# The filter stage of a Hyena and MoE kernel: a turned input, matrix B in an idle half, float32 row tiles, and an earlier first layer

## The chip, the cores and the metric

The kernel runs on one core of one Trainium2 chip. The metric is device time in microseconds (us) of one launch; the kernel before takes 2395.51 us, the median of 3 runs (2389.8 to 2403.55). Engines are named as in the profile: PE is TensorE (its weight loads, PEld, are shown apart), DVE VectorE, ACT ScalarE, POOL GpSimd, and SP the queue that issues most DMAs.

## The reference

Two layers follow each other, and both are computed in float32:

```python
h_mlp = np.maximum(pos_emb @ w1, 0.0) @ w2            # the filter: (S,64) @ (64,64), relu, @ (64,128)
h_filt = h_mlp * np.exp(-0.01 * pos)[:, None]
u = x * v                                             # (4, 11456, 128)
y = irfft(rfft(u, n=2*S) * rfft(h_filt, n=2*S)[None])[:, :S]
out1 = x * y                                          # 45824 tokens of 128
...
e_idx = argmax(out1 @ w_gate + modality_bias[modality_id])
out[token] = gate_w * (relu(out1 @ w1[e_idx]) @ w2[e_idx])      # 8 experts, 128 -> 1024 -> 128
```

The change touches only how the spectrum of `h_filt` is made, and when the first of the four batches of `x` and `v` is read.

## The kernel before, in words

The long convolution is done as a transform in two steps over N1 = 90 and N2 = 64 points. Everything is written as matrix products with constant tables. The program has these stages, in order:

1. **Filter, outer step** (16 steps q, `filter_stages`). A tile of `pos_emb` is loaded (`emb`), turned by four transposes (`pT`, L499) and copied to SBUF by ACT (`pTs`, L501); `hidden` multiplies by `w1` (`m1`, L507), and DVE applies relu and window (`r`, L510); `transform` does the outer transform with the table `whole` (`s`, L520), and ACT copies the result into `A[:, 0]` (L524). The second layer `w2` is not yet applied, since it acts on features and commutes with the transform.
2. **Filter, middle step** (30 groups g of G = 3 frequencies, `filter_middle`). `turn` transposes three slices of `A[:, 0]` (`pa`, L547), ACT copies them (`aT`, L549). `spectrum` multiplies by the table B of the group (`b2`, loaded by SP at L542; result `pz`, L556). Each half of the 128 rows of `pz` holds one of two blocks. ACT rounds both halves (L563) and DVE subtracts (L565), so that `z` holds for each block the rounded part in 64 partitions and the remainder in the other 64. `second` applies `w2` to both blocks with four float32r products (L572, L573) of full height against `ws`, a split of `w2`; ACT and DVE form the three rows of the filter's spectrum `h` (L577, L578, L579), and POOL's queue writes them to `hs` in HBM (L580, 384 KB a group).
3. **Forward step of batch 0** (16 steps q, `forward_stages`): SP loads a tile of `x` and one of `v` (`seq`, L447, 512 KB each); DVE forms `u = x*v` and the sum and difference of its halves (`product`: L452, L455, L456); PE transforms (`s`, L480, here with both blocks in one product of 128 rows); ACT copies into both halves of `A` (L482).
4. The middle step of batch 0 (`middle_stages`, from L615 on), then for each later batch the inverse step of the batch before, routing and the forward step together. From batch 1 on the forward product is done on two halves of 64 rows (L471).
5. The mixture of experts, tile by tile, to the end.

Order of work: PE, ACT, DVE and SP execute in the order in which the program is written. `steps(count, stages)` builds a list of steps from a table such as `"load:0 transform:4 turn:1 hidden:2"`: stage s of item i is written in step i + s, and inside a step in the table's order. `overlapped(first, second, n)` lays the last n steps of one list over the first n of the next. FOUT is the table of stage 1, FMID of stage 2, OUTER of the forward step; F1 = 1 and F2 = 2 are the overlaps between stages 1 and 2, and 2 and 3.

Buffers: `new_a` hands out the next of NA = 11 slots of 4 KB a partition, in turn; who gets a slot waits until its last user is done. Stage 1 takes three slots a step (`emb`, `pTs`, `r`), stage 2 three a group (`b2`, `aT`, `z`), stage 3 two a step (x and v). `ring("h")`, `ring("b")` and `ring("c")` give three places each in the tile `rings`. So `h` of group g waits until the write to `hs` of group g-3 has landed. `bank` gives one of four PSUM banks, `pair` one of two pairs of banks. `A` has two halves; during stages 1 and 2 the kernel before uses only `A[:, 0]`.

## Time and profile before

| what | value |
|---|---|
| median of 3 runs | 2395.51 us (2389.8 to 2403.55) |
| the profiled execution's own time | 2370.12 us |
| its span, first to last instruction | 2367.9 us |
| mean granted TensorE clock | 0.977 |
| PE busy in the span | 95% |
| filter, outer step | 0 to 49.57 us |
| filter, middle step | 49.57 to 120.86 us |
| forward step of batch 0 | 120.86 to 163.74 us |
| the rest | 163.74 to 2367.9 us |

How to read it: the page's shares are of the whole span; the change lies in its first 164 us, which are read with the timeline (instructions in order of time, equal neighbours merged into one row with their count), with the table of windows (busy time of each engine between two times) and with the list of waits. In a timeline row stand the start, the duration of the whole row, engine, line, operation, result<-operands, shape and count, and in brackets how long the engine was idle before and what ended that. A float32 product of PE shows as two records, a float32r product or a transpose as one.

### The profile page before, as it was taken

The page shows a single profiled execution, that of the slowest core. Times are in us where ns is not written, and L with a number is a line of the kernel's source. Part 1 is how long each engine was busy: PE and PEld are TensorE (multiplying, and loading weights), DVE is VectorE, ACT ScalarE, POOL GpSimd, SP SyncE. Part 2 cuts the span into 40 slices and gives each one's busy share as a digit, 9 for nine tenths or more (in the row PEclk, how much of TensorE's full clock was granted, in tenths as well). Part 3 has the DMA queues.
Part 4 walks back from the last instruction along what each step waited for, and adds up shares of the span by engine and source line. Part 5 has one row for each costly group of instructions (what it writes and reads, how often), then busy time and mean ns, then how long its engine had stood idle before and what let it go on. Part 6 is the DMA issues. An engine that isn't in the chain of part 4 may idle for free. (4 is left out here: it accounts for less than half of the span.)

```text
span 2367.9 us, 44124 instructions
## 1 busy us (share of the span) xinstructions
PE 2238.2 (95%) x14826; PEld 1874.1 (79%) x14826; DVE 1839.2 (78%) x3197; ACT 1515.7 (64%) x2969; POOL 994.7 (42%) x987
## 2 busy tenths in 40 slices
PE   8899999899989999899888999999999999999998
PEld 8789966798669966698446777777878888888898
DVE  3789888897788978797566777777777877777797
ACT  5757677577556766576445666666666666666676
POOL 0305400376435755276652554445444333333333
PEclk9999999999899999899998999999999999999999
DMA  3976667677867788575556722112221111111111
GB/s 114 314 298 197 220 223 223 185 226 260 288 209 227 225 285 298 183 222 174 174 163 184 246 68 72 61 62 74 67 62 60 59 46 45 45 46 46 39 41 34
DMA packets 188751, 359.04 MB, mean 152 GB/s; under 512 B 33937, under 2 KB 120285, under 8 KB 188521
## 3 DMA queue, kind: packets, MB, share of 16 engines
q1 hardware_dynamic: 161753, 296.77, 39.5%
q0 software_dynamic: 26608, 59.36, 7.4%
q8 instruction: 120, 1.97, 0.3%
q14 instruction: 110, 0.90, 0.1%
q10 hardware_dynamic: 160, 0.03, 0.0%
HBM read 271.63 MB, written 84.83 MB: 151 GB/s over the span
## 5 line engine op out<-in xcount | busy, mean ns | idle before, releaser
L1072 DVE SCALAR_TENSOR_TENSOR hl<-ph,hh 128x512 fp32r<-128x512 f32 x724 | 499.1, 689 | 249.7 <-ACT hh L1071 147.7
L1071 ACT ACTIVATE hh<-ph 128x512 fp32r<-128x512 f32 x724 | 434.0, 600 | 376.1 <-PE ph L1068 232.1
L1108 POOL DMA_INDIRECT out<-ot,idx x362 | 357.8, 988 | 651.3 <-DVE ot L1105 568.1
L264 POOL DMA_INDIRECT xs<-back,to x360 | 379.6, 1054 | 230.6 <-DVE y L701 81.3
L1066 PE MATMUL ph<-xh,wh 128*128 128x512 f32 (+1 forms) x792 | 304.0, 384 | 2.9 <-ACT wh L1037 2.9
L1089 PE MATMUL po<-hh,wh 128*128 128x512 f32 (+1 forms) x792 | 303.5, 383 | 0.0
L1068 PE MATMUL ph<-xl,wh 128*128 128x512 f32 (+1 forms) x792 | 295.7, 373 | 0.1
L1091 PE MATMUL po<-hl,wh 128*128 128x512 f32 (+1 forms) x792 | 294.9, 372 | 0.0
L1067 PE MATMUL ph<-xh,wl 128*128 128x512 f32 (+1 forms) x792 | 294.5, 372 | 0.0
L1090 PE MATMUL po<-hh,wl 128*128 128x512 f32 (+1 forms) x792 | 293.9, 371 | 0.0
L641 POOL TENSOR_TENSOR more<-more 128x384 f32<-128x384 f32 x112 | 112.4, 1004 | 278.0 <-DVE more L638 233.9
L647 DVE TENSOR_TENSOR part<-pz,rings 128x768 f32<-128x768 f32 x240 | 217.6, 948 | 0.0
L664 PE MATMUL pw<-rings,yT 128*128 128x128 f32 x1440 | 184.4, 279 | 5.4 <-DMA rings<-in_c_bc 5.4
L628 PE MATMUL pz<-rings,aT 128*128 128x128 f32 x1440 | 184.4, 279 | 3.9 <-ACT aT L616 2.3
L664 PEld LDWEIGHTS pw<-rings,yT 128*128 128x128 f32 x1440 | 174.4, 196 | 6.0 <-issue 6.0
L628 PEld LDWEIGHTS pz<-rings,aT 128*128 128x128 f32 x1440 | 174.3, 196 | 5.3 <-ACT aT L616 3.0
L687 PEld LDWEIGHTS wt<-ident,A 128*90 128x90 f32 x1024 | 124.1, 185 | 61.6 <-issue 26.2
L1068 PEld LDWEIGHTS ph<-xl,wh 128*128 128x128 f32 x792 | 149.5, 189 | 27.4 <-DVE xl L1053 0.3
L1091 PEld LDWEIGHTS po<-hl,wh 128*128 128x128 f32 x792 | 149.2, 188 | 27.0
L1066 PEld LDWEIGHTS ph<-xh,wh 128*128 128x128 f32 x792 | 149.7, 189 | 26.3 <-ACT wh L1037 3.3
L1067 PEld LDWEIGHTS ph<-xh,wl 128*128 128x128 f32 x792 | 150.0, 189 | 24.1 <-DVE wl L1038 0.4
L652 POOL TENSOR_TENSOR part<-part,more 128x384 f32<-128x384 f32 x112 | 122.2, 1091 | 110.0 <-DVE part L651 83.1
(186 smaller groups left out, 4426.9 us busy)
## 6 DMA issues: line engine op xcount, KB each, us to landing
seq<-in_x SPq DMA_DIRECT2D x128, 512.0 KB
rings<-in_c_bc SPq DMA_DIRECT2D x240, 192.0 KB
rings<-hs SPq DMA_DIRECT2D x120, 384.0 KB
seq<-in_v SPq DMA_DIRECT2D x64, 512.0 KB
xr<-xo SPq DMA_DIRECT2D x64, 365.6 KB
back<-xr SPq DMA_DIRECT2D x72, 325.0 KB
x<-xs SPq DMA_DIRECT2D x82, 260.0 KB
hs<-rings POOLq DMA_DIRECT2D x30, 384.0 KB
```

Source lines behind the costliest of these rows:

```text
L264: s = pool.indirect_dma_start(out=xs, out_offset=bass.IndirectOffsetOnAxis(ap=ix, axis=0), in_=src, in_offset=None, bounds_check=E * R - 1 ...
L628: pe.matmul(zv[:, blk, :, j], k["aT"][:, blk, D * j:D * j + D], k["b"][:, j, :], start=True, stop=True)
L664: pe.matmul(pw[:, 2 * N2 * j:2 * N2 * (j + 1)], k["yT"][:, blk, D * j:D * j + D], k["c"][:, j, :], start=True, stop=True)
L1066: pe.matmul(p, k[0, "h"][:, f:f + D], k["xh"], start=True, stop=False)
L1067: pe.matmul(p, k[0, "l"][:, f:f + D], k["xh"], start=False, stop=False)
L1068: pe.matmul(p, k[0, "h"][:, f:f + D], k["xl"], start=False, stop=True)
L1071: act.activation(hh, ph, AF.Relu)
L1072: dve.scalar_tensor_tensor(hl, ph, 0.0, hh.bitcast(F32), op0=ALU.max, op1=ALU.subtract)
L1089: pe.matmul(po, k[1, "h"][:, f], hh[:, t], start=g == 0, stop=False)
L1090: pe.matmul(po, k[1, "l"][:, f], hh[:, t], start=False, stop=False)
L1091: pe.matmul(po, k[1, "h"][:, f], hl[:, t], start=False, stop=g == NCH - 1)
L1108: s = pool.indirect_dma_start(out=out, out_offset=bass.IndirectOffsetOnAxis(ap=k["idx"][:, j:j + 1], axis=0), in_=ot[:, j, :], in_offset=N ...
```

## The change

1. `pos_emb` is laid out on the host so that each tile arrives turned. `turn` of stage 1, its four transposes and ACT's copy are gone; `hidden` reads `emb` itself. A step takes two slots instead of three, and the stages move one step closer (FOUT).
2. B of group g is loaded into `A[0:128, 1]`, the half of `A` that is idle in stages 1 and 2, by `load_b(g)`, which is written in step g of the whole program, so it starts with the first step of stage 1. `aT` and `z` live in the rings "b" and "c". Stage 2 takes no slot of `new_a` any more.
3. `second` is two plain float32 products, each with 64 rows: block m uses partitions 64m to 64m+63 of `w2` (it stands in `wf` twice) and of `z`. ACT copies `pz` once over 128 partitions; the split by DVE and the tile `ws` are gone.
4. In FMID the stages of a group stand at steps 0, 1 and 3 instead of 2, 3 and 5 (the load at 1 is gone).
5. The forward step of batch 0 uses the new table FIRST, laid over the last 18 steps of stage 2 (F2 = 18): loads from step 0, `product` 16 and `forward` 17 steps later.

The diff:

```diff
-FOUT = "load:0 transform:4 turn:1 hidden:2"
-FMID = "turn:2 spectrum:3 second:5 load:1"
+FOUT = "load:0 hidden:2 transform:3"
+FMID = "turn:0 spectrum:1 second:3"
+FIRST = "forward:17 load:0 product:16"
...
-F1, F2, F3 = 1, 2, 1
+F1, F2, F3 = 1, 18, 1
...
-        ws = keepp.tile([D, 2, D], F32R, name="ws")
...
-            act.copy(ws[:, 0], wf[:, 0])
-            dve.tensor_sub(ws[:, 1], wf[:, 0], ws[:, 0].bitcast(F32))
...
-            def turn(q):
-                t = kept.pop((q, "emb"))
-                pT = bank("pT")
-                for i in range(4):
-                    pe.transpose(pT[:, D * i:D * i + D], t[:, D * i:D * i + D], ident)
-                pTs = kept[q, 0] = new_a("pTs")[:, 0:512]
-                act.copy(pTs, pT)
-
             def hidden(q):
-                pTs = kept.pop((q, 0))
+                t = kept.pop((q, "emb"))
                 m1 = bank("m1")
                 for i in range(4):
-                    pe.matmul(m1[:, D * i:D * i + D], pTs[:, D * i:D * i + D], wf[:, 1],
+                    pe.matmul(m1[:, D * i:D * i + D], t[:, D * i:D * i + D], wf[:, 1],
                               start=True, stop=True)
...
+        def first_b(g):
+            return A[0:2 * N2, 1].rearrange("p (g j) c n -> p g j (c n)", j=G)[:, g]
+
+        def load_b(g):
+            sp.dma_start(first_b(g),
+                         a["c_bc"][g, :, 0:2 * GK].rearrange("p (j d) -> p j d", j=G))
...
-            def load(g):
-                t = kept[g, "b"] = new_a("b2")[0:2 * N2, 0:2 * GK].rearrange(
-                    "p (j d) -> p j d", j=G)
-                sp.dma_start(t, a["c_bc"][g, :, 0:2 * GK].rearrange("p (j d) -> p j d", j=G))
...
-                aT = kept[g, "aT"] = new_a("aT")[0:2 * N2, 0:G * D]
-                act.copy(aT, pa[0:2 * N2, 0:G * D])
+                aT = kept[g, "aT"] = ring("b")
+                act.copy(aT, pa[:, 0:G * D])
...
-                z = kept[g, "z"] = new_a("z", F32R)[:, 0:4 * GK].rearrange(
-                    "p (b m) -> p b m", b=2)
-                halves = slice(0, 64), slice(64, D)
-                for blk, at in enumerate(halves):
-                    act.copy(z[at, blk], pz[at, 0:2 * GK])
-                for blk, at in enumerate(halves):
-                    dve.tensor_sub(z[halves[1 - blk], blk], pz[at, 0:2 * GK],
-                                   z[at, blk].bitcast(F32))
+                z = kept[g, "z"] = ring("c")
+                act.copy(z, pz[:, 0:2 * GK])
...
                 for m in range(2):
-                    pe.matmul(ph[:, m, 0:2 * GK], ws[:, 0], z[:, m], start=True, stop=False)
-                    pe.matmul(ph[:, m, 0:2 * GK], ws[:, 1], z[:, m], start=False, stop=True)
+                    at = slice(64 * m, 64 * m + 64)
+                    pe.matmul(ph[:, m, 0:2 * GK], wf[at, 0], z[at], start=True, stop=True)
...
-            table = [w.split(":") for w in (LAST if b == nb else OUTER).split()]
+            table = [w.split(":") for w in (LAST if b == nb else OUTER if b else FIRST).split()]
...
         seq = overlapped(steps(NQ, filter_stages()), steps(NG, filter_middle()), F1)
+        for k in range(NG):
+            seq[k] = lambda f=seq[k], k=k: (f(), load_b(k))
...
-        pos.transpose(3, 2, 1, 4, 0, 5).reshape(NQ, D, -1))
+        pos.transpose(3, 0, 5, 4, 2, 1).reshape(NQ, D, -1))
```

How the rows of the engines' orders move, at the three places that matter. First SP, from the program's start: before, 16 loads of `emb` with the constants between, then 30 loads of B, then `seq` (x and v in turn).

```order
L493 DMA emb<-in_pos_emb 128x512 x5
L396 DMA fwd<-in_c_fwd 128x360
L397 DMA inv<-in_c_inv 90x128
L398 DMA small<-in_c_small 128x634
L399 DMA wg<-in_moe_w_gate 128x8
L400 DMA bias<-in_moe_modality_bias 128x16
L493 DMA emb<-in_pos_emb 128x512 x11
L542 DMA b_510<-in_c_bc 128x384
L542 DMA b_518<-in_c_bc 128x384
```

Now the last of `emb`, the end of B and the first of x and v; ahead of these rows `emb` and `A` alternate from the first instruction on.

```order
L490 DMA emb<-in_pos_emb 128x512
L528 DMA A<-in_c_bc 128x384
L490 DMA emb<-in_pos_emb 128x512
L528 DMA A<-in_c_bc 128x384 x15
L444 DMA seq<-in_x 128x1024
L444 DMA seq<-in_v 128x1024
```

B no longer waits behind all of `emb`, and the first x stands right behind the 30th B; it waits for a slot of `new_a`, and 11 such loads find slots that only stage 1 has used.

Second PE, one group in the middle of stage 2, before (`pa` is the turn, `pz` the spectrum, `ph` the second layer):

```order
L547 MATMUL pa<-ident,A 128x128 x3
L556 MATMUL pz<-b_552,aT 128x128 x3
L572 MATMUL ph<-z,ws 128x384
L573 MATMUL ph<-z,ws 128x384
L572 MATMUL ph<-z,ws 128x384
L573 MATMUL ph<-z,ws 128x384
```

and now, with the start of the next group:

```order
L539 MATMUL pa<-ident,A 128x128 x3
L548 MATMUL pz<-A,rings 128x128 x3
L559 MATMUL ph<-rings,wf 128x384 x2
L539 MATMUL pa<-ident,A 128x128 x3
L548 MATMUL pz<-A,rings 128x128 x3
```

Four products of `ph` became two; turn and spectrum stand as they stood.

Third DVE, at the end of stage 2, before (L578 and L579 belong to `second`, L452, L455 and L456 to `product` of the forward step):

```order
L578 TENSOR_TENSOR rings<-ph,rings 128x192
L579 TENSOR_TENSOR rings<-ph,rings 128x192
L452 TENSOR_TENSOR seq<-seq 128x1024
L455 TENSOR_TENSOR seq<-seq 128x512
L456 TENSOR_TENSOR seq<-seq 128x512
```

and now:

```order
L564 TENSOR_TENSOR rings<-ph,rings 128x192
L565 TENSOR_TENSOR rings<-ph,rings 128x192
L449 TENSOR_TENSOR seq<-seq 128x1024
L452 TENSOR_TENSOR seq<-seq 128x512
L453 TENSOR_TENSOR seq<-seq 128x512
L564 TENSOR_TENSOR rings<-ph,rings 128x192
L565 TENSOR_TENSOR rings<-ph,rings 128x192
L449 TENSOR_TENSOR seq<-seq 128x1024
```

The first product stands one group earlier: behind group 28, ahead of group 29, the last.

More of the change, by code (lines that the diff above doesn't have):

```diff
@@ L493, in load, with hidden @@
                 sp.dma_start(t, a["pos_emb"][q])
-            def turn(q):
+            def hidden(q):
                 t = kept.pop((q, "emb"))
-                pT = bank("pT")
-                for i in range(4):
-                    pe.transpose(pT[:, D * i:D * i + D], t[:, D * i:D * i + D], ident)
-                pTs = kept[q, 0] = new_a("pTs")[:, 0:512]
-                act.copy(pTs, pT)
-            def hidden(q):
-                pTs = kept.pop((q, 0))
                 m1 = bank("m1")
                 for i in range(4):
-                    pe.matmul(m1[:, D * i:D * i + D], pTs[:, D * i:D * i + D], wf[:, 1],
+                    pe.matmul(m1[:, D * i:D * i + D], t[:, D * i:D * i + D], wf[:, 1],
                               start=True, stop=True)
@@ L525, in transform @@
                              p[:, h, 0:4 * N1].rearrange("p (n k) -> p k n", n=2))
-            todo = dict(turn=turn, hidden=hidden, transform=transform, load=load)
+            todo = dict(hidden=hidden, transform=transform, load=load)
             return [(int(t), todo[n]) for n, t in (w.split(":") for w in FOUT.split())]
@@ L547, in turn @@
                     pe.transpose(pa[0:2 * N2, D * j:D * j + D], turn_back(g, 0, j), ident)
-                aT = kept[g, "aT"] = new_a("aT")[0:2 * N2, 0:G * D]
-                act.copy(aT, pa[0:2 * N2, 0:G * D])
+                aT = kept[g, "aT"] = ring("b")
+                act.copy(aT, pa[:, 0:G * D])
             def spectrum(g):
-                aT, b2 = kept.pop((g, "aT")), kept.pop((g, "b"))
+                aT, b2 = kept.pop((g, "aT")), first_b(g)
                 pz = bank("pz")
@@ L581, in second @@
                                h[:, :, 1:3].rearrange("p m c k -> p m (c k)"))
-            todo = dict(turn=turn, second=second, spectrum=spectrum, load=load)
+            todo = dict(turn=turn, second=second, spectrum=spectrum)
             return [(int(t), todo[n]) for n, t in (w.split(":") for w in FMID.split())]
@@ L863, in outer_steps @@
                                lambda: (send(NO - 1), places(NO - 1))])
-            table = [w.split(":") for w in (LAST if b == nb else OUTER).split()]
-            return steps(NQ, [(lambda q, t=int(t): min(q + t, NQ + 3) if b < nb else q + t, todo[n])
+            table = [w.split(":") for w in (LAST if b == nb else OUTER if b else FIRST).split()]
+            return steps(NQ, [(lambda q, t=int(t): min(q + t, NQ + 3) if 0 < b < nb else q + t, todo[n])
                               for n, t in table if n in todo])
```

## The prediction

> **What bounds the kernel now.** I read the windows of the first stages, then the timeline of each, then the waits. The table of windows gives, by stage: length, busy time and count for PE, PEld, DVE, ACT, POOL, then granted clock, DMA share and GB/s.
>
> ```profile
> 0.00:49.57 49.57, 43.91 (x320) 43.15 (x321) 11.87 (x21) 23.02 (x51) 3.20 (x11) 1.00 0.40 118
> 49.57:103.48 53.91, 51.04 (x357) 46.77 (x358) 44.12 (x101) 45.24 (x107) 15.54 (x23) 1.00 0.83 260
> 103.48:120.86 17.38, 6.74 (x35) 5.07 (x34) 9.80 (x23) 6.08 (x14) 4.72 (x7) 0.77 1.00 376
> 120.86:163.74 42.88, 42.01 (x256) 41.67 (x256) 36.97 (x46) 25.55 (x32) 0.00 (x0) 0.94 0.92 356
> ```
>
> PE is nearly always busy in the outer step, in most of the middle step and in the forward step. In the third row it is busy for 6.74 of 17.38 us, the DMA engines are full, and the clock falls to 0.77. Here x and v are first read:
>
> ```profile
> 103.34 0.33 SPq L447 DMA_DIRECT2D seq<-in_x  x1
> 115.71 0.33 SPq L447 DMA_DIRECT2D seq<-in_x  x1
> ACT rings L577 <- DMA hs<-rings: 13.3, 12, 2.8
> L580 POOL DMA_DIRECT2D hs<-rings x30: 671/677/688, 57.7 to 119.5; - x30
> 103.48 0.67 POOL L580 DMA_DIRECT2D hs<-rings  x1 [1.14 <-ACT z L563]
> ```
>
> Eleven loads start from 103.34 to 115.71. The 30 writes of h leave between 57.7 and 119.5; the one at 103.48 is the 24th, so 23 intervals before it are 1.99 us each and the 6 after it 2.66 us. ACT's copy for h waits 13.3 us in total for an older write, since h has three places.
>
> From 163.74 us on nothing is changed and what follows starts when the forward step ends; PE is 95% busy over the whole span, so I carry a shift there in full to the end. The profiled execution took 2370.12 us, 25.4 (1.1%) less than the median of the runs, 2395.51. I sum in microseconds against the execution and subtract the same amount from the median.
>
> **Part 1: the outer step loses its turn.**
>
> ```profile
> 6.69 2.04 PE L507 MATMUL m<-wf,pTs 128*128 128x128 f32 x8 [1.10 <-DMA wf<-in_w]
> 10.76 1.39 PE L520 MATMUL s<-bs,r 128*128 128x180 f32 x8
> 11.98 0.60 PE L499 MATMUL pT<-ident,emb 128*128 128x128 f32 x4
> 12.41 1.06 PE L507 MATMUL m<-wf,pTs 128*128 128x128 f32 x8
> 13.31 1.39 PE L520 MATMUL s<-bs,r 128*128 128x180 f32 x8
> 14.53 0.60 PE L499 MATMUL pT<-ident,emb 128*128 128x128 f32 x4
> 46.05 2.61 PE L520 MATMUL s<-bs,r 128*128 128x180 f32 x16
> 49.57 0.88 PE L547 MATMUL pa<-ident,A 128*128 128x128 f32 x6 [0.91 <-ACT A L524]
> ```
>
> A step takes 2.55 us (11.98 to 14.53) and PE does not pause in it: 0.43 of turns (11.98 to 12.41), 0.90 of hidden (12.41 to 13.31), 1.22 of transform (13.31 to 14.53). Without turns 2.12 us remain. ACT (23 us of 49.57 busy) and DVE (12) are far from this, so nothing else takes the time up. At the start nothing is gained: the first product waits for w1 until 6.69, and runs at half pace (2.04 us for what later takes 1.06). The first two hidden products then take some 3.6 us, and the first transform starts near 10.3 instead of 10.76. Fourteen steps of 2.12 and two transforms of 1.22 lead to 42.4; with the 1.1 us from there to the first turn of the middle step (48.5 to 49.57 now) that one starts at 43.5: **-6.1 us**. Bounds: -7.0 (16 times 0.43) if the start costs nothing; -4.4 if PE runs at half pace for one more 3.4 us, because the transposes that now precede 6.69 are gone.
>
> SP now sends B, 5.9 MB, in the same time. The first row's 118 GB/s over 49.57 us are 5.8 MB; together 11.7 MB in 42 us, 280 GB/s, within the 260 at a share of 0.83 of the second row. So PE should not wait for `emb`.
>
> **Part 2: the middle step.** One group now:
>
> ```profile
> 77.60 0.45 PE L572 MATMUL ph<-z,ws 128*128 128x384 f32 x1
> 78.41 0.49 PE L547 MATMUL pa<-ident,A 128*128 128x128 f32 x3
> 78.73 0.83 PE L556 MATMUL pz<-b,aT 128*128 128x128 f32 x6
> 79.41 0.44 PE L572 MATMUL ph<-z,ws 128*128 128x384 f32 x1
> ```
>
> 1.81 us of PE without a pause: second 0.81, turn 0.32, spectrum 0.68. The 1.99 achieved is this plus waits for writes of h. Turn and spectrum stay, 1.00. The four one-record products become two float32 products of 64 rows, four records. Their price is not in this stage; the nearest rows are the 64-row products of batch 1 and their neighbours:
>
> ```profile
> 320.24 2.01 PE L687 MATMUL wt<-ident,A 128*90 128x128 f32 x16
> 322.18 2.02 PE L471 MATMUL s<-fwd,seq 64*128 64x90 f32 x32
> 324.25 0.94 PE L744 MATMUL xT<-ident,xo 109*128 109x109 f32 x8
> 325.12 1.94 PE L696 MATMUL py<-rings,inv 90*64 90x512 f32 x8
> 326.99 0.94 PE L752 MATMUL pl<-rings,wg 128*32 128x436 f32 x8
> ```
>
> A record of 180 columns and full height starts every 0.153 us (1.22 / 8), one of 128 every 0.112 (0.90 / 8): 0.79 ns a column, so 0.082 for 90 columns and 0.315 for 384. The 64-row records of 90 columns come 32 in 2.07 us, 0.065 each, less than 0.082: the two halves do run at the same time. L696, two halves of columns, does 8 records of 512 in 1.87 us, where 0.415 each would be 3.3. So a group's second layer costs between 2 x 0.315 = 0.63 (full overlap) and 4 x 0.315 = 1.26 (none). I take 0.63. Around such a burst time is lost: L687 to L471 takes 1.94 us where 16 steps of 0.112 are 1.79, L471 to L744 2.07 where 16 pairs at 0.112 are 1.79; 0.43 together. I charge that to each group: 1.00 + 0.63 + 0.43 = 2.06 us, more than PE's 1.81 now, and a little more than the 1.99 achieved.
>
> The Trainium skill has a rule that speaks against this edit: TensorEngine Tiling (Array Packing), section Key Properties, says that a change of tiling mode drains TensorE. The rows above agree in that a change costs something, 0.43 us for going in and out, less than a third of a burst's own time there. By the page's speedup of up to 2x alone, without the drain, the group would be 1.63 us and the total some 12 us lower.
>
> Will writes of h still bound it? The chain of one place:
>
> ```profile
> 55.35 0.48 ACT L577 COPY rings<-ph 128x384 f32<-128x384 f32 x1
> 57.73 0.69 POOL L580 DMA_DIRECT2D hs<-rings  x1 [53.52 <-ACT rings L577]
> 61.16 0.48 ACT L577 COPY rings<-ph 128x384 f32<-128x384 f32 x1 [0.62 <-DMA hs<-rings]
> 115.07 0.36 DVE L578 TENSOR_TENSOR rings<-ph,rings 128x192 f32<-128x192 f32 x1 [1.20 <-ACT rings L577]
> 115.34 0.35 DVE L579 TENSOR_TENSOR rings<-ph,rings 128x192 f32<-128x192 f32 x1
> ```
>
> From copy to copy 5.81 us for three groups, 1.94. 2.38 of it lie between copy and POOL's issue, because DVE is at its split (L565, gone now). Unhindered, copy to end of the last DVE row takes 1.1 us, and POOL follows 0.6 later: 5.1 us, 1.70 a group, and B's traffic is gone too. So PE, at 2.06, decides. ACT has three copies of 0.48 a group (1.44), DVE 0.7: both hidden.
>
> x and v: stage 1 takes 32 slots, so the first eleven loads get slots that are freed by its steps 9 to 15. They are behind B and done 15.3 us (5.77 MB at 376 GB/s) after B, near 52 us (11.7 MB at the second row's 260 / 0.83 take 37 us), while the first h is written near 50. The collision of the third row thus all but disappears.
>
> The first second-layer product comes some 4.0 us after the first turn, at 47.5; group 26 follows at 101.1 (26 x 2.06), and since the turns and then the spectra run out, group 28 at 103.9 (one spectrum and two bursts of 1.06 later). Its products take 1.06, and copy and DVE follow in 1.6 (the 1.1 above and an estimated 0.5 until ACT starts): 106.6. From the first turn that is 63.1 us; today 115.69 (115.34 + 0.35) - 49.57 = 66.1: **-3.0 us**. The bounds of this part are the prices of the second layer; they are rivals A and C.
>
> **Part 3: the forward step starts earlier behind it.**
>
> ```profile
> 118.31 0.36 DVE L578 TENSOR_TENSOR rings<-ph,rings 128x192 f32<-128x192 f32 x1 [2.62 <-ACT rings L577]
> 118.84 1.22 DVE L452 TENSOR_TENSOR seq<-seq 128x1024 f32<-128x1024 f32 x1
> 120.89 42.01 PE L480 MATMUL s<-fwd,seq 128*128 128x180 f32 x256 [5.25 <-issue]
> 121.30 1.22 DVE L452 TENSOR_TENSOR seq<-seq 128x1024 f32<-128x1024 f32 x1
> 163.74 1.53 PE L615 MATMUL aT<-ident,A 128*128 128x128 f32 x12 [0.85 <-ACT A L482]
> ```
>
> Today the first product stands behind group 29, whose h waits 2.6 us for a write; it does not wait for x or v. Then PE needs 42.0 us where 256 records at 0.1525 are 39.0: 3.0 are lost to the clock of 0.77 that the idle time brought. From group 28's h (115.69) to 163.74 it is 48.05 us. Now the product starts directly behind group 28. PE starts 2.0 after it, and DVE becomes the pace, 2.46 a step (118.84 to 121.30) against 2.44 of PE, with group 29 (0.6) between steps 0 and 1: 0.6 + 15 x 2.46 + 2.0 + 2.44 + 0.84 = 42.8. **-5.2 us**. Bounds: -8 if DVE hides too (41.9) and PE's short wait costs nothing, -2.2 if the wait of about 2.6 us before the first forward product halves the clock as now.
>
> **Sum:** -6.1 - 3.0 - 5.2 = -14.3 us: 2356 for the execution, **2381 us** for the median.
>
> **Rivals.**
> *A, the halves do not overlap.* Overlap at 384 columns is inferred from 90 columns, where 0.065 is nearer to a full 0.082 than to half of it. Then a group costs 2.69, 29 x 0.63 = +18.3 us, and the kernel is 4.0 us slower: 2400. The gain is gone from 2.55 us a group on (2.06 + 14.3/29). For it: the weak ratio; against: L696's clean one.
> *B, loads of x and v still meet the writes.* If they come in the middle of the stage, some 6 groups (15.3 us) take 2.66 instead of 2.06, and the pause halves the clock again: +3.6 +3.0, 2388. For it: SP must first bring all of B. This is also the case in which the early loading does not do what it says.
> *C, the change of mode is hidden* by loads of weights and other work, and the chain of writes at 1.70 decides: 29 x 0.36 = -10.4 us, 2371. Against: both gaps around L471.
>
> **How the numbers follow.** Forecast 0.60 (2377 to 2386 by the bounds of parts 1 and 3), A 0.08, B 0.19, C 0.13. A measurement here can tell about 0.5%, 12 us, from no change. Of the forecast 0.43 lies below 2383.5, C lies there wholly, of B 0.02: faster 0.58. A is slower, but only part of it, with a costlier change of mode, by 12 us: 0.03. The rest is the same: 0.39. The range leaves out the far parts of A and C: 2369 to 2396.
>
> **What would show it.** Right: `hidden` every 2.12 us; the first turn near 43.5; second-layer records in pairs and a group every 2.0 to 2.1 us; no wait of ACT for `hs` above 1 us; x and v landed by 55 us; the first forward product near 109 and L601 near 149 instead of 163.74. Wrong: a group above 2.5 us (A), writes of h spaced by 2.6 us (B), 1.7 us (C), or a shift at 149 that is not found at the end.

## The result and the profile after

The changed kernel takes 2375.2 us, the median of 7 runs (2370.33 to 2378.34); the kernel before, timed beside it, takes 2395.51 (median of 7, 2386.92 to 2403.55). The ratio is 0.992, 95% interval 0.9898 to 0.9941: 0.8% faster, 20.3 us by the medians. The forecast was 2381 with a range of 2369 to 2396, so the change did what was forecast, and by these medians 6 us more. Two later comparisons put it at 0.994 (0.9918 to 0.9962) and 0.9933 (0.991 to 0.9956).

The two profiled executions say something else if only their ends are read: 2374.49 us now against 2370.12 before, 4.4 us more. Where the time went has to be read stage by stage. The table of windows of the changed kernel, cut at its own stage ends (first turn of the middle step, h of group 28 done, first turn of batch 0), with the columns as before:

```profile
0.00:45.18 45.18, 37.02 (x257) 36.80 (x257) 11.67 (x20) 14.83 (x34) 3.20 (x11) 1.00 0.84 285
45.18:105.97 60.79, 59.77 (x390) 39.98 (x390) 18.02 (x59) 41.31 (x89) 18.57 (x28) 1.00 0.63 238
105.97:150.07 44.10, 41.48 (x259) 40.70 (x257) 39.40 (x51) 26.14 (x33) 1.70 (x3) 0.96 0.85 324
```

Before, the same three pieces were 49.57, 66.12 (to 115.69) and 48.05 us. So they became 4.4, 5.3 and 4.0 us shorter, 13.7 together; 14.3 were forecast, as 6.1, 3.0 and 5.2. PE is busy for 59.8 of 60.8 us in the middle step, and the starved stretch in which the clock fell to 0.77 is gone. The lines that answer to those of before, from the timeline of PE:

```profile
7.16 3.75 PE L496 MATMUL m<-wf,emb 128*128 128x128 f32 x16 [7.16 <-DMA wf<-in_w]
10.70 2.61 PE L509 MATMUL s<-bs,r 128*128 128x180 f32 x8
15.32 1.05 PE L496 MATMUL m<-wf,emb 128*128 128x128 f32 x8
17.43 1.05 PE L496 MATMUL m<-wf,emb 128*128 128x128 f32 x8
45.18 0.84 PE L539 MATMUL pa<-ident,A 128*128 128x128 f32 x6 [1.00 <-ACT A L513]
61.40 0.92 PE L559 MATMUL ph<-rings,wf 64*128 64x384 f32 x4
62.25 0.55 PE L539 MATMUL pa<-ident,A 128*128 128x128 f32 x3
62.63 0.83 PE L548 MATMUL pz<-A,rings 128*128 128x128 f32 x6
63.40 0.92 PE L559 MATMUL ph<-rings,wf 64*128 64x384 f32 x4
107.94 41.28 PE L477 MATMUL s<-fwd,seq 128*128 128x180 f32 x256 [1.75 <-ACT rings L563]
150.07 1.53 PE L601 MATMUL aT<-ident,A 128*128 128x128 f32 x12 [0.85 <-ACT A L479]
```

An outer step takes 2.11 us (15.32 to 17.43), a group 1.99 to 2.00 (61.40 to 63.40). From the waits and from the timelines of ACT and SP:

```profile
ACT rings L563 <- DMA hs<-rings: 6.2, 6, 1.9
57.63 0.48 ACT L563 COPY rings<-ph 128x384 f32<-128x384 f32 x1 [1.89 <-DMA hs<-rings]
106.85 0.48 ACT L563 COPY rings<-ph 128x384 f32<-128x384 f32 x1 [1.52 <-DMA hs<-rings]
29.46 7.77 SPq L528 DMA_DIRECT2D A<-in_c_bc  x15
37.44 0.33 SPq L444 DMA_DIRECT2D seq<-in_x  x1
45.95 0.33 SPq L444 DMA_DIRECT2D seq<-in_x  x1
```

ACT waits 6.2 us in all for writes of h, where it waited 13.3. B is issued by 37.2 us, and the eleven early loads of x and v are issued from 37.44 to 45.95, before the middle step writes its first h at 51.84. They take longer to arrive: the DMA engines still move 390 GB/s from 54 to 56 us, and 21 from 58 to 60. So the first three writes do meet them, which is the wait of 1.89 us at 57.63.

### The profile page after: what moved, and what is told of

It is laid out like the page before. It is cut to its first block, busy times and chain, and to the rows that moved or that the text cites. A ratio compares the mean times of both kernels' runs of the same rounds, so it can differ in the third digit from the quotient of the medians.

```text
span 2372.7 us, 43805 instructions
## 1 busy us (share of the span) xinstructions
PE 2233.0 (94%) x14762; PEld 1853.4 (78%) x14762; DVE 1805.4 (76%) x3136; ACT 1499.0 (63%) x2922; POOL 995.5 (42%) x987
## 3 DMA queue, kind: packets, MB, share of 16 engines
q8 instruction: 119, 1.95, 0.3%
## 5 line engine op out<-in xcount | busy, mean ns | idle before, releaser
L674 ACT COPY rings<-wt 90x512 f32<-90x512 f32 x256 | 140.3, 595 | 46.4 <-PE wt L673 19.4
```

## The experiments

Theory: the gain is made in the first 150 us and carried to the end. In these 150 us it comes from the turns that are gone, and from x and v being read before the writes of h instead of among them; the row tiles themselves gain nothing. Rivals: that the row tiles bring it; that the new table FIRST brings the loads forward; that later stages gain or lose too.

The runs came in three groups, each on one chip with the kernel before timed beside it: median 2393.84 us for the first four runs, 2311.18 for the next four, 2366.32 for the last four. Times are therefore compared inside a group, as ratios to its own kernel before. "First turn" is the first transpose of the middle step, "batch 0" the first transpose of batch 0, both in the profile of the run, in us; what each run is stands below. one_half, which computes another result, and split_b, which gives out fewer slots, are read in the profile only; the ratio of the change is that of the first comparison.

| run | first turn | batch 0 | between | ratio to before (95%) |
|---|---|---|---|---|
| before | 49.57 | 163.74 | 114.2 | |
| before_again | 50.28 | 166.02 | 115.7 | 0.9999 (0.9974 to 1.0025) |
| turned | 43.75 | 158.03 | 114.3 | 0.9958 (0.9932 to 0.9985) |
| rows | 43.45 | 158.70 | 115.3 | 0.999 (0.9967 to 1.0013) |
| late_xv | 43.62 | 150.65 | 107.0 | 0.9948 (0.9923 to 0.9973) |
| the change | 45.18 | 150.07 | 104.9 | 0.992 (0.9898 to 0.9941) |
| after_again | 44.25 | 148.88 | 104.6 | 0.994 (0.9918 to 0.9962) |
| after_third | 42.76 | 147.99 | 105.2 | 0.9933 (0.991 to 0.9956) |
| one_half | 43.00 | 165.86 | 122.9 | |
| split_b | 44.42 | 148.61 | 104.2 | |
| merged5 | 44.15 | 152.27 | 108.1 | 0.996 (0.9947 to 0.9974) |
| best | 42.24 | 151.21 | 109.0 | 0.9955 (0.9936 to 0.9974) |
| merged_xo | 43.30 | 141.51 | 98.2 | 0.9912 (0.988 to 0.9944) |
| best2 | 42.97 | 141.84 | 98.9 | 0.9907 (0.9875 to 0.994) |

### What one profiled execution is worth

before_again is the kernel before, with no edit.

> The kernel before, unchanged, profiled a second time. It tells how far one profiled execution stands for the median. Theory (the time before is the same work each time, and the profiled execution of before, 2370 us against a median of 2396, was a lucky one in its late stages): the first 164 us repeat to within 0.3 us (first turn of the middle step at 49.6, first turn of batch 0 at 163.7), the end differs by 5 us or more from 2367.9, and the ratio to the kernel before is 1.000. Rival (the profiled execution is always some 25 us faster than the timed ones): the span is again 2368 within 3 us.

Its span is 2387.7 us, 19.8 more than that of the first profile. The theory's "to within 0.3 us" for the first 164 us was too narrow: the first turn came 0.7 us later and batch 0 2.3 us later. After that the two executions drift apart: by products of the middle steps (`pw`) the second is 2.3 us behind at 174 us, 5.2 ahead at 782, 11.8 ahead at 1058, and by products of the experts (`po`) 4.9 ahead at 1262, 8.3 behind at 1569 and 17.6 behind from 1870 on. So identical work drifts by 20 us over the late stages, more than the whole change. That the changed kernel's profiled execution ends 4.4 us later than the first one before is of this kind: it was 13.7 us ahead at batch 0 and 17.7 ahead at 1114 us, lost 11 of these by the start of the experts (1262 us), most of it in the last inverse step, and 11 more in their first half.

after_again and after_third are the changed kernel, with no edit.

> The changed kernel, unchanged, profiled and timed once more. Identical work differed by up to 20 us from 300 us on between the two profiled executions of the kernel before, while the first 280 us agreed within 2.3 us. Theory (the change is worth what the filter and the first forward step show, 13 to 15 us, and the 20 us of the first comparison of medians are that and the scatter of executions): first turn of the middle step at 43.5 to 45.2 (w1 arrives between 6.0 and 7.2 us), first turn of batch 0 within 1.5 us of 149.5, median 12 to 17 us below before. Rival (the late stages gain too, since what follows meets transfers differently): batch 0 at 149.5 and the median 18 to 23 us below.

> The changed kernel once more, as the measure for the two versions timed beside it. The two comparisons so far gave 20 and 14 us below before, the second one the sum of the prediction. Theory (the front's 13.5 to 15 us, carried to the end): ratio 0.9935 to 0.9945, 12.5 to 15.5 us. Rival (the late stages gain as well): 18 us or more.

By the medians 2296.85 against 2311.18 (14.3 us) and 2353.34 against 2366.32 (13.0 us; 15.9 by the ratio). The three ratios, 0.992, 0.994 and 0.9933, average 0.9931, 16 to 17 us. In the profiles batch 0 starts at 149.0 on average (three executions) against 164.9 (two), 15.9 us earlier. The rival, late stages that gain as well, isn't needed.

### One part at a time

turned has the turned `pos_emb` alone:

```diff
-FOUT = "load:0 transform:4 turn:1 hidden:2"
+FOUT = "load:0 hidden:2 transform:3"
...
-            def turn(q):
...
-                pTs = kept.pop((q, 0))
+                pTs = kept.pop((q, "emb"))
...
-        pos.transpose(3, 2, 1, 4, 0, 5).reshape(NQ, D, -1))
+        pos.transpose(3, 0, 5, 4, 2, 1).reshape(NQ, D, -1))
```

> Of the change, only the turned pos_emb: outer step of two stages, B still loaded in the middle step into slots, second layer still four float32r products, x and v as before. Theory (the parts add up; the outer step is worth 16 x 0.43 us less what the late clock at the start takes): steps of 2.11 us, half clock until about 13.3 us, first turn of the middle step at 45.2 instead of 49.57; from there everything as before, so the first turn of batch 0 at 159.3 instead of 163.74 and the median 4.4 us lower (ratio 0.998). Rival 1 (the late clock has to do with the early traffic of B, not with the missing turns): first turn at 42.6 to 43.5, batch 0 at about 157. Rival 2 (the middle step waits for something that did not move): batch 0 at 163 again, median unchanged.

The first turn comes at 43.75, between the theory's 45.2 and the rival's 42.6 to 43.5, 5.8 us before the kernel before; batch 0 comes 5.7 us before it. All of the outer step's gain is passed on by the middle step (the median is 7.9 us lower, with an interval of 3.6 to 16 us by the ratio). On the first product the rival is wrong, though: in the runs that load B early as well the first turn lies anywhere from 42.76 to 45.18, so it isn't B's early traffic that decides it (below).

rows adds the row tiles and the rings, but loads B in the middle step:

```diff
-FMID = "turn:0 spectrum:1 second:3"
-FIRST = "forward:17 load:0 product:16"
+FMID = "turn:1 spectrum:2 second:4 load:0"
+FIRST = "forward:2 load:0 product:1"
...
-F1, F2, F3 = 1, 18, 1
+F1, F2, F3 = 1, 2, 1
...
+            def load(g):
+                t = kept[g, "b"] = new_a("b2")[0:2 * N2, 0:2 * GK].rearrange(
+                    "p (j d) -> p j d", j=G)
+                sp.dma_start(t, a["c_bc"][g, :, 0:2 * GK].rearrange("p (j d) -> p j d", j=G))
...
-                aT, b2 = kept.pop((g, "aT")), first_b(g)
+                aT, b2 = kept.pop((g, "aT")), kept.pop((g, "b"))
...
-        for k in range(NG):
-            seq[k] = lambda f=seq[k], k=k: (f(), load_b(k))
```

> The change without B in A's half and without the new place of the forward step: turned pos_emb, two float32 products of 64 rows, aT and z in rings, but B of each group still loaded in the middle step into slots, so that x and v stand behind it on SP. Theory (a group of row tiles takes PE 1.99 us, no less than the 1.99 that the writes of h allowed before, and what the middle step gained came from moving x and v away from the writes of h): first turn at 45.2, groups 1.99 apart until x and v are read near 100 us, then 2.6 us apart again, the clock halved before the forward step for about 10 us, first turn of batch 0 at 158 to 160, median 4 to 7 us lower than before. Rival (the row tiles themselves bring it, since without the split on DVE a write of h is issued earlier after its copy, and the chain of three places is short enough to bear the reads of x and v): groups stay at 2.0 to the end, batch 0 at 150 to 153, median 11 to 14 us lower.

From its timelines (SP, POOL, PE), its waits and its windows:

```profile
71.41 8.30 SPq L539 DMA_DIRECT2D b<-in_c_bc  x5
81.38 0.33 SPq L444 DMA_DIRECT2D seq<-in_x  x1
85.94 0.68 POOL L571 DMA_DIRECT2D hs<-rings  x1 [1.32 <-ACT rings L556]
114.64 0.68 POOL L571 DMA_DIRECT2D hs<-rings  x1 [1.59 <-ACT rings L568]
117.03 40.82 PE L477 MATMUL s<-fwd,seq 128*128 128x180 f32 x256 [3.39 <-issue]
ACT rings L568 <- DMA hs<-rings: 17.7, 11, 2.3
85.94:114.64 28.70, 20.44 (x111) 11.37 (x109) 6.40 (x21) 11.00 (x26) 6.75 (x10) 0.92 0.95 336
```

The theory holds on what bounds the stage. x and v are read from 81.38 us on, earlier than the 103.34 of before and than the expected 100, because stage 2 now leaves slots free. The last B has been issued by 79.7, so it is not B that they meet but the writes of h: the ten intervals from 85.94 to 114.64 are 2.87 us on average, ACT waits 17.7 us for writes, and the DMA engines are at 0.95 in this stretch. From first turn to batch 0 it takes 115.3 us, no less than before (114.2). Here the shorter chain of copy and write did not help. The earlier batch 0 (158.70) isn't found at the end: the ratio is 0.999, 4 to 7 us were expected, and the interval allows up to 8.

late_xv is the changed kernel with the old place of the forward step:

```diff
-FIRST = "forward:17 load:0 product:16"
+FIRST = "forward:2 load:0 product:1"
...
-F1, F2, F3 = 1, 18, 1
+F1, F2, F3 = 1, 2, 1
```

> The changed kernel with the forward step of batch 0 laid over only two steps of the filter again, as before; B stays in A's idle half. SP's order of transfers is then the same as in the changed kernel, only the first product of DVE and the first transform of PE stand behind the last group instead of ahead of it. Theory (what frees the transfers of x and v is that SP has no B to load in the middle step; the place in the order is worth one group on DVE): the loads of x and v still begin near 37.5 us, groups 1.99, first turn of batch 0 about 1 to 3 us later than the 150.07 of the changed kernel, median 1 to 3 us above it. Rival (the early place is what brings the loads forward): loads begin after 95 us, writes of h 2.6 us apart at the end, batch 0 at 156 or later.

x is read from 35.91 us on although the table is the old one, and between first turn and batch 0 lie 107.0 us, against 104.6 to 105.2 in the three profiles of the changed kernel. So what brings the loads forward is that SP has no B to load any more in the middle step; the new table only puts one product of DVE ahead of group 29, which is worth some 2 us by this one profile. Its batch 0 starts 0.6 us after that of the changed kernel's first profile, with a first turn that was 1.6 us earlier.

### The price of the row tiles

In one_half both products of a group use partitions 0 to 63: block 0 is computed twice and block 1 left out.

```diff
-                    at = slice(64 * m, 64 * m + 64)
+                    at = slice(0, 64)
```

> The changed kernel with both second-layer products of a group on partitions 0 to 63 of w2 and z: block 0 is computed twice and block 1 is left out, so that the two products have the same tile of 64 rows and cannot run side by side. Everything else is the same. Theory (the two halves run at the same time in the changed kernel, 0.63 us of a group's 1.99): four records of 384 columns one after the other, 0.315 us each, second layer 1.26, group 2.6 us, the middle step 18 us longer, first turn of batch 0 near 168. Rival (the records of 64 rows are cheaper than full ones, and side by side or not makes no difference): group 1.99 us, batch 0 near 150.

Its PE timeline:

```profile
68.00 1.55 PE L559 MATMUL ph<-rings,wf 64*128 64x384 f32 x4
69.48 0.55 PE L539 MATMUL pa<-ident,A 128*128 128x128 f32 x3
69.87 0.83 PE L548 MATMUL pz<-A,rings 128*128 128x128 f32 x6
70.63 1.55 PE L559 MATMUL ph<-rings,wf 64*128 64x384 f32 x4
```

A group takes 2.63 us (68.00 to 70.63) instead of 1.99: the two halves run side by side in the changed kernel, and the 0.64 us that this saves are the 2 x 0.315 of the prediction. Its end isn't comparable: without block 1 the filter is another one, and tokens can go to other experts.

split_b keeps B in A's half and has the second layer of before, which it writes ahead of the spectrum inside a step:

```diff
-FMID = "turn:0 spectrum:1 second:3"
+FMID = "turn:0 second:3 spectrum:1"
...
-NA, NXO = 11, 3
+NA, NXO = 9, 3
...
+        ws = keepp.tile([D, 2, D], F32R, name="ws")
+        z_t = [keepp.tile([D, 4 * GK], F32R, name=f"zt{i}") for i in range(2)]
...
-                z = kept[g, "z"] = ring("c")
-                act.copy(z, pz[:, 0:2 * GK])
+                z = kept[g, "z"] = z_t[g % 2].rearrange("p (b m) -> p b m", b=2)
+                halves = slice(0, 64), slice(64, D)
+                for blk, at in enumerate(halves):
+                    act.copy(z[at, blk], pz[at, 0:2 * GK])
+                for blk, at in enumerate(halves):
+                    dve.tensor_sub(z[halves[1 - blk], blk], pz[at, 0:2 * GK],
+                                   z[at, blk].bitcast(F32))
...
-                    pe.matmul(ph[:, m, 0:2 * GK], wf[at, 0], z[at], start=True, stop=True)
+                    pe.matmul(ph[:, m, 0:2 * GK], ws[:, 0], z[:, m], start=True, stop=False)
+                    pe.matmul(ph[:, m, 0:2 * GK], ws[:, 1], z[:, m], start=False, stop=True)
```

> The changed kernel with the second layer of before: four float32r products of full height, z split by ACT and DVE, in two tiles of its own; to make room, nine slots instead of eleven are given out in the first part of the program, so that later stages and the total aren't comparable. B lies in A's idle half, pos_emb is turned. Only the middle step of the filter is read. Theory (the row tiles are not what gained: PE needs 1.81 us for the old group and 1.99 for the new, and before, writes of h that met B and x and v set the pace): groups 1.81 to 1.95 us apart, so the middle step ends up to 5 us earlier than with row tiles. Rival (the split on DVE, 2.38 us between the copy of h and its write, keeps the old form at 1.99 or above even without B's transfers): 1.99 to 2.3 us a group.

Of its timelines, POOL and then DVE:

```profile
65.80 0.67 POOL L575 DMA_DIRECT2D hs<-rings  x1 [1.15 <-ACT rings L545]
95.28 0.67 POOL L575 DMA_DIRECT2D hs<-rings  x1 [1.15 <-ACT rings L545]
98.77 1.14 DVE L559 TENSOR_TENSOR zt<-pz,zt 64x384 fp32r<-64x384 f32 x2
99.94 0.36 DVE L573 TENSOR_TENSOR rings<-ph,rings 128x192 f32<-128x192 f32 x1
100.22 0.35 DVE L574 TENSOR_TENSOR rings<-ph,rings 128x192 f32<-128x192 f32 x1
100.59 1.14 DVE L559 TENSOR_TENSOR zt<-pz,zt 64x384 fp32r<-64x384 f32 x2
```

The 17 writes from 65.80 to 95.28 leave 16 intervals of 1.84 us on average (1.82 or 1.83 but for two); no copy waits for a write. With x, v and B out of the way the old form is the faster one in the middle of the stage, 1.82 against 1.99. The row tiles cost 0.17 us a group. Whether PE or DVE sets the 1.82 isn't separated: from 65.80 to 95.28 PE is busy for 29.41 and DVE for 27.70 of 29.48 us. The old form loses most of its lead at the end, where the turns run out: it is then still held by DVE (1.82 a group, 98.77 to 100.59), while the last writes of the changed kernel leave 1.7 and 0.9 us apart (103.94, 105.65, 106.50). From first turn to batch 0 the two take 104.2 and 104.9 us, where up to 5 us had been expected. So the row tiles made room for z; they are not what makes the middle step fast.

### Fewer changes of mode

If a group of 1.99 is 1.00 of turn and spectrum, 0.63 of two halves side by side, and 0.36 for going into the tiled form and out of it, then two groups in one burst (products of the second layer with no other product between them) pay it once. merged5 does that, with two more places of h in A's second half from group 10 on:

```diff
-FMID = "turn:0 spectrum:1 second:3"
+FMID = "turn:0 spectrum:1 second:2"
...
             def second(g):
...
+                if g % 2 == 0:
+                    return
+                two = [pair("ph") for _ in range(2)]
+                for k in range(2):
+                    z = kept.pop((g - 1 + k, "z"))
+                    for m in range(2):
+                        at = slice(64 * m, 64 * m + 64)
+                        pe.matmul(two[k][:, m, 0:2 * GK], wf[at, 0], z[at], start=True, stop=True)
+                for k in range(2):
+                    finish(g - 1 + k, two[k])
...
-                hf = ring("h")
+                spare = A[:, 1].rearrange("p k c n -> p (k c n)")
+                h_at = [r for r in ring_of["h"][0]] + [spare[:, 6 * GK * i:6 * GK * i + 6 * GK] for i in range(2)]
+                hf = h_at[g % 5] if g >= 10 else h_at[g % 3]
```

> The changed kernel with the second layer of two groups in one burst, every second group (eight records of 64 rows together instead of four and four), so that the change of mode is paid 15 times and not 30; h gets five places instead of three, since two copies now come at once. Theory (what a group of 1.99 holds beside 1.00 of turn and spectrum and 0.63 of the halves is a change of mode of some 0.36 us, paid per burst): two groups in 2 x 1.63 + 0.36 = 3.6 us, a group 1.81, the middle step 30 x 0.18 = 5.4 us shorter than in the changed kernel, the median 5 us below it. Rival (the 1.99 is set by something else, ACT's copies or POOL's issue of the writes): groups stay at 1.99 on average, no gain, or a loss since the copies of h come in pairs and wait for one another.

Undisturbed pairs did take 3.64 us, but the kernel is not 5 us faster: its median is 2302.34 against 2296.85 for the changed kernel beside it. It lost more than it gained, at two places. From its PE timeline:

```profile
73.04 0.94 PE L548 MATMUL pz<-A,rings 128*128 128x128 f32 x6 [1.36 <-ACT rings L541]
105.19 2.68 PE L477 MATMUL s<-fwd,seq 128*128 128x180 f32 x16 [1.87 <-issue]
111.67 13.53 PE L477 MATMUL s<-fwd,seq 128*128 128x180 f32 x68 [3.80 <-ACT A L479]
```

At 73.04 (and, for 2.01 us, at 56.77) PE waits for ACT, which is held at a copy of h: up to group 9 there are only three places, and group 10 takes the one that group 9 has just filled. And the forward step stops for 3.8 us after its first 16 records. By the edit, its copies into A must wait until the last writes out of A's second half are done, an effect of the borrowed place that the expectation had overlooked; merged_xo below, with the places elsewhere, doesn't have this stop. best adds 24 transposes ahead of w1's arrival:

```diff
+        pw = bank("warm")
+        for k in range(24):
+            pe.transpose(pw[:, D * (k % 4):D * (k % 4) + D], ident, ident)
+        act.copy(warm[:, 0:1], pw[0:1, 0:1])
```

> As the pair bursts with five places of h, and in addition 24 transposes of the identity on PE ahead of everything (their result isn't used; they are added work), ended before w1 arrives. Theory (the granted clock of PE is low until PE was busy for some 3.4 us, so that the 16 records that follow w1's arrival run at half pace because the turns that stood there are gone): the first product at w1's arrival runs at full or nearly full pace, the first transform 1.5 to 2 us after it instead of 3.5, first turn of the middle step 2 to 3 us earlier than without (41 to 42.5), the median 7 us below the changed kernel. Rival (the clock rises at a fixed time after the start, whatever PE does): first turn as without them, 43.5 to 45.2.

With them the 16 records behind w1 take less time:

```profile
2.52 4.40 PE L871 MATMUL warm<-ident 128*128 128x128 f32 x24 [2.52 <-POOL ident masks.py:199]
6.76 1.95 PE L496 MATMUL m<-wf,emb 128*128 128x128 f32 x16
9.06 1.46 PE L509 MATMUL s<-bs,r 128*128 128x180 f32 x8 [0.35 <-DMA bs<-in_c_whole]
```

1.95 us instead of 3.75, and the first turn is at 42.24, 1.9 before merged5. The middle step loses part of it again, and the median, 2301.20, is that of merged5 and not the expected 7 us below the changed kernel. merged_xo is merged5 with the two places in tiles that are first used at the first inverse step:

```diff
-                spare = A[:, 1].rearrange("p k c n -> p (k c n)")
-                h_at = [r for r in ring_of["h"][0]] + [spare[:, 6 * GK * i:6 * GK * i + 6 * GK] for i in range(2)]
-                hf = h_at[g % 5] if g >= 10 else h_at[g % 3]
+                h_at = ring_of["h"][0] + [t.rearrange("p a b c r -> p (a b c r)")[:, 0:6 * GK]
+                                          for t in xo_t[:2]]
+                hf = h_at[g % 5]
```

> The second layer of two groups in one burst as in the pair-burst run before, whose undisturbed pairs took 3.63 us (1.82 a group against 1.99). That run lost it again, because two of its five places of h lay in the second half of A: the forward step's first copies into A waited 6.9 us, and PE 3.8 us. Here these two places lie in tiles that are first used at the first inverse step. Theory (those waits were the whole loss): 3.63 us a pair from the start of the stage, no wait of the forward step, first turn of batch 0 at 144 to 146, median 4 to 5 us below the changed kernel. Rival (the paired copies of h and the transfers of x and v disturb each other at the start, where that run waited 3.4 us for ACT, whatever the places): first turn of batch 0 at 147 to 149, median within 2 us of the changed kernel.

> The same with the 24 added transposes ahead of w1's arrival, which brought the first turn of the middle step from 44.15 to 42.24 us. Theory (the two gains add): first turn near 42, first turn of batch 0 at 142 to 144, median 6 to 7 us below the changed kernel. Rival (an earlier middle step meets more of the transfers of x and v and gives the 2 us back): median as for the pair bursts alone.

merged_xo's PE timeline:

```profile
65.43 1.56 PE L562 MATMUL ph<-rings,wf 64*128 64x384 f32 x8
69.07 1.56 PE L562 MATMUL ph<-rings,wf 64*128 64x384 f32 x8
72.70 1.56 PE L562 MATMUL ph<-rings,wf 64*128 64x384 f32 x8
100.35 40.31 PE L477 MATMUL s<-fwd,seq 128*128 128x180 f32 x256 [1.87 <-issue]
141.51 1.53 PE L610 MATMUL aT<-ident,A 128*128 128x128 f32 x12 [0.85 <-ACT A L479]
```

Pairs are 3.63 to 3.64 us apart from the start, ACT doesn't wait for a write at all, and batch 0 starts at 141.51, 98.2 us after the first turn: 6.7 less than in the changed kernel, better than the 144 to 146 expected. Some 5 of these are the groups (30 x 0.17), and 1.0 is a forward step of 40.31 us instead of 41.28: here both groups of the last pair stand between the first two products of DVE, so PE starts 0.6 us closer to the second one, and DVE's last step lacks a wait of 0.4. The clock is not the reason (see part 3 below). The median is 2343.21 against 2353.34 for the changed kernel beside it, 10 us less; 6.5 of these are there at batch 0 (147.99 in after_third). The ratios to before are 0.9912 and 0.9933 and their intervals overlap, so that the gain is clearer in the profile than in the total. What five places of h do without the paired bursts was not run; in the changed kernel PE is busy for 59.8 of 60.8 us of this stage, which leaves them at most 1 us. best2, with the added transposes, gives 2345.84 and a ratio of 0.9907, which is no different. Its first turn came at 42.97, only 0.3 before merged_xo's: in that execution the transposes themselves were still running when w1 had come,

```profile
2.53 5.38 PE L871 MATMUL warm<-ident 128*128 128x128 f32 x24 [2.53 <-POOL ident masks.py:199]
7.70 2.17 PE L496 MATMUL m<-wf,emb 128*128 128x128 f32 x16
```

since the clock rose later (8.15 us, and 5.76 in best). That busy PE ahead of w1 can gain 1.9 us is shown by best; that it does so on average is not.

## Why the prediction was right, point by point

That the sum of this pair of profiles, 13.7 us, comes so near to 14.3 is in part luck: the three parts miss by +1.7, -2.3 and +1.2 us, and the misses cancel. The mechanisms are taken one by one.

- **Part 1, the outer step.** The step of 2.12 us is 2.11. The first turn was forecast at 43.5 (-6.1; bounds -7.0 to -4.4). The profiled execution of the change has 45.18, the lower bound; the ten executions of kernels with this outer step and no added transposes lie between 42.76 and 45.18, 43.8 on average, and the two of before are at 49.57 and 50.28: 6.1 us. The step that was treated too simply is the start: "the first transform starts near 10.3". It started between 9.57 (after_third) and 10.70 and ran at half or full pace, because w1 arrives between 6.03 and 7.16 us, and the clock rises 2.9 to 6.1 us after that.
- **Part 2, the middle step.** 1.00 + 0.63 + 0.43 = 2.06 was forecast, 1.99 measured. All three terms are shown: overlap by one_half (0.64 us more without it), and a price that is paid once per burst by the paired bursts (3.63 for two groups, so 2 x 1.63 + 0.37). 0.43 was mis-sized by 0.07: the row of before charged the edges of another burst. Over 26 groups that is 1.8 of the 2.3 us by which this part came out better (-5.3 instead of -3.0). The forecast that PE decides held too. In split_b the old products run at 1.82 a group, so that PE needs no more than this for them, and row tiles made the group dearer.
- **The collision of x, v and h** "all but disappears": right in the main, and rows shows that without B's new place it stays (2.87 us a group). Two of the signs did not come as written. x and v were to be landed by 55 us, and they fill the DMA engines until about 57. And no wait of ACT for `hs` was to exceed 1 us: besides the 1.89 us at 57.63, the copy of the last group waits 1.5 us in all three profiles of the changed kernel (at 106.85 in the first), since the last groups follow each other faster than the three places come free. Neither holds PE up: it is busy for 59.8 of 60.8 us in the stage, and its first forward product (107.94) starts when L452 of the first step is done (107.83).
- **The price of a burst.** The rule that the prediction weighed, that a change of tiling mode drains TensorE (the Trainium skill, TensorEngine Tiling (Array Packing), section Key Properties), agrees with this case: going into the 64-row products and out of them costs 0.36 to 0.37 us a burst. The runs show this price, and that it is paid per burst; that a drain is what takes the time is not shown apart.
- **Part 3, the forward step.** -5.2 was forecast, -4.0 measured (44.10 us from h of group 28 to batch 0, 42.8 forecast). The order of DVE is as forecast, with 2.46 us a step at first. In the changed kernel's first profile the clock does halve for one window of 3.4 us behind the short wait (the bound of -2.2 let it stay halved as long as before). Clock windows:

```profile
102.05:105.47 3.42, 2.69 (x18) 1.68 (x18) 1.36 (x5) 1.92 (x4) 1.24 (x2) 1.00 0.46 169
105.47:108.88 3.41, 1.65 (x8) 0.78 (x7) 3.38 (x7) 0.48 (x1) 1.35 (x2) 1.00 0.78 282
108.88:112.29 3.41, 3.41 (x14) 3.41 (x13) 3.38 (x5) 0.79 (x1) 0.67 (x1) 0.50 0.79 272
112.29:115.70 3.41, 3.41 (x24) 3.41 (x23) 3.34 (x6) 2.26 (x3) 0.00 (x0) 1.00 0.65 208
```

  In the window after one with 1.65 of 3.41 us of busy PE the clock is 0.50, and after a full window it is 1.00 again. But this is not what part 3 had left out. In after_third the same wait falls over two windows and the clock stays at 1.00, and the forward step takes the same 41.28 us:

```profile
101.42:104.84 3.42, 1.98 (x12) 0.73 (x8) 2.18 (x5) 1.15 (x4) 1.75 (x3) 1.00 0.52 194
104.84:108.25 3.41, 2.37 (x14) 2.13 (x15) 3.34 (x7) 1.03 (x2) 0.94 (x2) 1.00 0.89 286
105.87 41.28 PE L477 MATMUL s<-fwd,seq 128*128 128x180 f32 x256 [1.74 <-ACT rings L563]
```

  DVE sets the pace, as forecast, and what PE loses in the halved window is hidden behind it. What was mis-sized are the terms of DVE. Its last rows in the first profile:

```profile
143.78 1.22 DVE L449 TENSOR_TENSOR seq<-seq 128x1024 f32<-128x1024 f32 x1
145.47 0.69 DVE L452 TENSOR_TENSOR seq<-seq 128x512 f32<-128x512 f32 x1 [0.46 <-DVE seq L449]
146.07 0.68 DVE L453 TENSOR_TENSOR seq<-seq 128x512 f32<-128x512 f32 x1
```

  From the first product (105.89) to the last it takes 37.9 us where 0.6 + 15 x 2.46 = 37.5 were forecast, since the steps are 2.53 us from 128.6 on. From the last product to batch 0 it takes 6.3 us where 2.0 + 2.44 + 0.84 = 5.3 were forecast: L452 waits 0.46 us, and the 2.44 us of PE count from the end of L453 (146.75), 0.6 us after that of L452, from which the 2.0 was read.
- **The shift is carried to the end.** Right on average: 15.9 us at batch 0, 16 to 17 us by the three ratios. In a single pair of executions it can't be seen.
- **Rivals.** A (no overlap) is excluded by one_half, B (x and v still meet the writes in the middle of the stage) by the loads at 37.44 and the groups of 1.99, C (a hidden change of mode at 1.70 a group) by the paired bursts. What the prediction did not say, and late_xv and split_b show, is which edits carry the gain: the turned input some 6 us, B's place, and with it the early reading of x and v, some 8 (107.0 instead of 115.3 between first turn and batch 0, late_xv against rows), FIRST some 2 (104.9 against 107.0), and the row tiles nothing (115.3 in rows against 114.3 in turned, 104.9 against 104.2 in split_b).

That the medians first showed 20 us and not 14 needs no missing mechanism: 2395.51 and 2375.2 each stand for seven executions of which single ones scatter by 17 and 8 us, and the two later comparisons gave 14.3 and 13.0.

## What to carry to other kernels

When several edits come together, price the one that only moves transfers apart from the one that changes products: here nearly all of the gain behind the outer step came from B's new place, which let x and v be read before the writes of h instead of among them, while the new products cost more time than the old. Here each burst of 64-row products cost 0.36 us at its edges, and joining two bursts saved one such price; the places that this needs must not be ones that the next stage writes first. Before a halved clock is blamed for lost time, look for an execution of the same kernel without it: here the forward step took 41.28 us with and without. If identical work drifts by 20 us between profiled executions, read a change of 15 us at the end of the stage that it touches, and use ends only as medians.

## What was not expected of the hardware

- In the traces the granted clock changes only on a grid of 3.41 us whose position differs between executions: in the changed kernel's first profile it rises at 13.30, is halved from 108.88 to 112.29 and from 276.13 to 279.54, and these are 28 and 77 steps of 3.413 us behind the first rise. That first rise lies at 9.28 to 13.30 us in the ten profiles with the turned input and no added transposes, 2.9 to 6.1 us after the first product. With PE kept busy from 2.5 us on it rises at 5.76 and 8.15 us. Together with w1's arrival (6.03 to 7.16 us), this moves the first turn between 42.76 and 45.18 from one execution to the next.
- Around the start of the forward step, grid windows of 3.41 us in which PE was busy for 1.53 (after_again), 1.54 (best2) and 1.65 us (the change) were each followed by a window at half clock; windows with 1.83 (one_half), 1.98 (after_third) and 2.11 us (merged_xo) were not. So the same short wait halves the clock in one execution and not in another, by where it falls on the grid.
- The same kernel takes 2393.84, 2311.18 and 2366.32 us (medians of 35, 21 and 25 runs) on the chips of the three groups, 3.6% apart, while batch 0 of the changed kernel starts within 2.1 us in its three profiles. The difference arises in the later stages: in the changed kernel's profiles PE is busy for 588 of 589 us from 1211 to 1800 us on the second chip, and for 596 of 618 from 1256 to 1874 in the first profile. What makes PE wait there stays open.
